# A dilated 15-tap convolution with gates: the taps split 2 apart as well, the products joined in PSUM, and a planned order

## The chip, the cores and the metric

The kernel runs on one core of one Trainium2 chip. The metric is the device time of one execution in microseconds, from the runs of the kernel by itself; beside them one execution was taken by the profiler, and the times of single instructions come from that one. The engines are named as in the profile: PE multiplies matrices (PEld is its load of the stationary operand), DVE does element-wise work, ACT applies functions and copies, POOL fills constants and issues some transfers, and SP issues most transfers.

## The reference

Cut to what is computed (two sequences of 16000 tokens with 144 channels; 15 taps, two tokens apart; all in bfloat16):

```python
B, T, D, K = (2, 16000, 144, 15)
pad = (K - 1) * 2
xp = jnp.pad(x, ((0, 0), (pad, 0), (0, 0)))
h = sum(einsum('btc,cd->btd', xp[:, pad - 2*i : pad - 2*i + T, :], w[i]) for i in range(K))
z = tanh(h[..., :D]) * sigmoid(h[..., D:])
return z @ w_o
```

Since the taps are two tokens apart, the even and the odd tokens are two sequences of their own, each with 15 neighbouring taps.

## The kernel before

**Tiling.** A stretch is 24 positions of one parity. A block is 64 stretches of both parities, which makes 128 rows: ten blocks and a half one. A unit is 12 of the 24 positions of the 128 stretches (`r` is 0 or 1), 21 units in all. For each unit the stationary operand of every matmul is a 128x128 piece of the input (128 channels by 128 stretches) and the moving one is a tap's weights, 128x288; the results stand in PSUM as 128 stretches by 288 outputs, two of them in an `acc` of two banks.

**Split taps.** The taps 8 apart are split in the manner of Karatsuba, so that the input appears as four streams, S (sum of two positions 8 apart), D (their difference) and E twice (the difference 16 apart, for the products that the code numbers 2 and 3). Each stream is split once more, 4 apart: `pe_V` makes a shared product with summed weights `H` (8 matmuls), `pe_A` makes the four others from the differences S4, D4 or E4 (`derive`). In each of these the 16 channels beyond 128 of up to eight taps are one more matmul, on `rx` and the weights `Wr`, `wrA` and `wrB`. That is 110 matmuls of 288 columns in a unit. ACT takes every product from PSUM to SBUF (`ev_V`, `act_ev`), and DVE adds the shared product to the others (`tt` with `bc`) and sums the products to `y`, for the last two products straight from PSUM.

**The rest of a unit.** `gate_act` and `gate_mul` make `z`. A transposing transfer on SP's queue makes `zT` of it (`start_zT`), and in the following unit PE multiplies it by `w_o` (`outproj`, four groups of 6 matmuls of 144 columns), ACT copies the groups to `os`, and SP stores them.

**Loads.** For a block SP issues four transposing loads (`load_x`: `xn` holds channels 0 to 127, `xb` channels 16 to 143), and then eight copies within SBUF that shift the last 16 channels of `xb` by 0 to 7 positions into `rx` (`load_r`).

**Order.** Every instruction stands in the order in which the code is written (`keep_in_program_order`). Weights come over ACT's queue (L191) and POOL's, and DVE makes their sums (L225 to L239). PE is kept busy with 54 matmuls on zeros (L218) until the first data are there. The transfers of SP and ACT take eight completion semaphores in turn (DMAHW0 to DMAHW7), those of POOL eight others (DMASW0 to DMASW7). A transfer is issued only after the earlier transfer on the same semaphore has landed, and while it waits, everything behind it on the issuing engine waits too. The first places of ACT's order are these; `[waits ...]` names the semaphores that end a wait:

```order
L191 DMA w_all<-in_w_dram 128x4x288 x3
L191 DMA w_all<-in_w_dram 128x3x288
L194 ACT_TABLE_LOAD
L194 ACTIVATE warm<-warm 128x1 [waits Pool_49]
L245 COPY H<-w_all 128x288 [waits DMAHW4_49]
L247 ACTIVATE Wr<-wrA 128x288 [waits DMASW0_49]
```

ACT issues four transfers here, none of which waits, and then goes over to its own work.

Of the kernel before, what the change touches and what calls it, by code (L numbers as in the profile page):

```python
# [8 lines left out]
BF16 = mybir.dt.bfloat16  # L9
# [4 lines left out]

@with_exitstack
def kernel(
# [7 lines left out]

    nc = tc.nc
    P = 128
# [3 lines left out]
    CM = 128  # L39
    CR = D - CM  # L40
    PU = 24
    NCL = 12
    HA = 16
    GAP = 32
    assert (B, T, D, K, D2) == (2, 16000, 144, 15, 288)
    TOT = 2 * T + GAP
    NBIG = 10
    BTOK = [3072] * NBIG + [1536]
    BT0 = [3072 * i for i in range(NBIG + 1)]
    NBLK = NBIG + 1  # L50
    assert BT0[-1] + BTOK[-1] >= TOT
    XW = HA + 1536 + 16
    ZW = 1792

# [4 lines left out]
    xa_pool = ctx.enter_context(tc.tile_pool(name="xa", bufs=2))  # L59
    d_pool = ctx.enter_context(tc.tile_pool(name="d", bufs=2))  # L60
    y_pool = ctx.enter_context(tc.tile_pool(name="y", bufs=2))
    c_pool = ctx.enter_context(tc.tile_pool(name="c", bufs=2))
    v_pool = ctx.enter_context(tc.tile_pool(name="v", bufs=4))
    g_pool = ctx.enter_context(tc.tile_pool(name="g", bufs=2))
    zt_pool = ctx.enter_context(tc.tile_pool(name="zt", bufs=2))
    os_pool = ctx.enter_context(tc.tile_pool(name="os", bufs=2))
    ps_acc = ctx.enter_context(tc.tile_pool(name="ps_acc", bufs=3, space=bass.MemoryType.PSUM))
    ps_out = ctx.enter_context(tc.tile_pool(name="ps_out", bufs=2, space=bass.MemoryType.PSUM))


    def segs(bi):

        t0 = BT0[bi] - 2 * HA
        t1 = BT0[bi] + BTOK[bi]
        loads, zeros = [], []
        marks = [(-2 * HA, 0, None, 0), (0, T, 0, 0), (T, T + GAP, None, 0), (T + GAP, TOT, 1, T + GAP),
                 (TOT, TOT + 1536, None, 0)]
        for (a, e, b, base) in marks:
            a_, e_ = max(a, t0), min(e, t1)
            if a_ >= e_:  # L80
                continue
            c0, c1 = (a_ - t0) // 2, (e_ - t0) // 2
            if b is None:
                zeros.append((c0, c1))
            else:
                loads.append((c0, b, a_ - base, c1 - c0))
        return loads, zeros

    def store_segs(bi):

        res = []
        p0, npd = BT0[bi] // 48, BTOK[bi] // 48
        for b in range(B):
            f0 = (b * (T + GAP)) // 48
            nfull, rest = T // 48, (T % 48) // 4
            a, e = max(f0, p0), min(f0 + nfull, p0 + npd)
            if a < e:
                res.append((a - p0, e - a, NCL, b, (a - f0) * 48))
            if rest and p0 <= f0 + nfull < p0 + npd:
                res.append((f0 + nfull - p0, 1, rest, b, nfull * 48))  # L100
        return res

    blocks = {}

    def load_x(bi, names=("xn", "xb")):
        loads, zeros = segs(bi)
        cur = blocks.setdefault(bi, dict(bi=bi))
        for nm in names:
            c0 = 0 if nm == "xn" else D - P
            t_ = xa_pool.tile([P, 2, XW], BF16, name=nm)  # L110
            cur[nm] = t_
            for (a, e) in zeros:
                K_(nc.gpsimd.memset(t_[:, :, a:e], 0.0))
            for e in range(2):
                for (col, b, tk, n) in loads:
                    src = bass.AP(x.tensor, x[b, tk + e, c0].offset, [[2 * D, n], [1, P]])
                    K_(nc.sync.dma_start_transpose(out=t_[:, e, col:col + n], in_=src))  # L117

    def load_r(bi, engs=None):
        engs = engs or (nc.sync,)  # L120
        cur = blocks[bi]
        cw = HA + BTOK[bi] // 2
        rx = xa_pool.tile([P, 2, XW], BF16, name="rx")
        for i in range(8):
            K_(engs[i % len(engs)].dma_start(out=rx[CR * i:CR * (i + 1), :, 8:cw], in_=cur["xb"][P - CR:P, :, 8 - i:cw - i]))  # L125
        cur["rx"] = rx

    def tt(out_, a, b, op):
        return K_(nc.vector.tensor_tensor(out=out_, in0=a, in1=b, op=op))  # L129


    GEO = {"S": (-8, 16), "D": (-8, 16), "E": (-16, 24), "S4": (-8, 12), "D4": (-8, 12), "E4": (-16, 20),
           "Sr": (0, 8), "Dr": (0, 8), "Er": (-8, 16)}

    def derive(bi, nm):
        cur = blocks[bi]
        big = bi < NBIG
        npd = BTOK[bi] // 48
        u0, wd = GEO[nm]
        t_ = d_pool.tile([P, GEO[nm][1] * P], BF16, name=nm)  # L140
        cur[nm] = t_

        def src(x_, u):

            s = u + HA
            v = x_[:, :, s:s + PU * npd]
            if big and wd == PU:
                return v
            return v.rearrange("p e (k j) -> p e k j" if big else "p e (k j) -> p j e k", j=PU)[
                (slice(None),) * (3 if big else 1) + (slice(0, wd),)]  # L150

        if nm in ("S4", "D4", "E4"):
            b = cur[nm[0]]
            bw = GEO[nm[0]][1]
            if big:
# [382 lines left out]
```

## Time and profile before

| | us |
|---|---|
| three runs by themselves | 354.19, 352.77, 353.88 (median 353.88) |
| span of the profiled execution | 352.6 |
| PE busy in it | 334.4 (95%) |
| weight loads on PE | 318.0 (90%) |
| DVE, ACT busy | 293.2 (83%), 220.8 (63%) |

The span of the profiled execution is 1.3 us below the median of the runs. A row of the groups view names the line, the engine, the operation, output and inputs, the shape and the count; behind the bar stand busy time, the mean of one in ns, and the idle time before. A row of the chain of waits has start, duration and what the chain ran through. `L267` is the line of every matmul and `L129` that of every DVE operation on two tensors, so their tiles tell them apart: `acc` is the convolution, `po` the output product.

### The profile page before, as it was taken

Reading aid. Unit: us, or ns where it says so; the run is one execution under the profiler, and the core shown is the slowest. Engines: PE = TensorE matmul, PEld = TensorE weight load, DVE = VectorE, ACT = ScalarE, POOL = GpSimd, SP = SyncE. Lnnn points to the kernel's source line nnn. Section 1 sums busy time; section 2 is a strip of 40 time slices with the busy share of each in tenths; the row PEclk is TensorE's granted clock in tenths of the full one; section 3 lists DMA queues with packets and bytes.
Section 4 is the critical chain, followed back from the end, with each engine's and each line's share of the span. In section 5 each row is a group of like instructions: output and inputs, shape, how many; then the busy total and the mean of one; then the engine's idle time right before and its main releaser. Section 6 shows DMA issues by size and latency. Waiting matters only on the chain.

```text
span 352.6 us, 7171 instructions
## 1 busy us (share of the span) xinstructions
PE 334.4 (95%) x2891; PEld 318.0 (90%) x2892; DVE 293.2 (83%) x393; ACT 220.8 (63%) x388; POOL 21.3 (6%) x48
## 2 busy tenths in 40 slices
PE   8938899999999999989999999989999999999994
PEld 3527799999999999989999999989999999999873
DVE  1826999789889888977988897878889889979984
ACT  2122567576765767657576765757676575776773
POOL 5255100000000000000000000000000000000002
PEclk9987999999999999999999999999999999999999
DMA  9998899969869787697997888698789865633224
GB/s 203 132 119 181 89 157 148 120 131 180 129 97 196 145 91 145 110 162 110 196 151 94 161 122 137 86 187 168 92 169 159 121 116 90 121 73 60 59 46 93
DMA packets 141881, 45.33 MB, mean 129 GB/s; under 512 B 136938, under 2 KB 139306, under 8 KB 141848
## 3 DMA queue, kind: packets, MB, share of 16 engines
q1 hardware_dynamic: 138588, 42.28, 73.6%
q0 software_dynamic: 1024, 1.43, 3.1%
q10 hardware_dynamic: 2236, 1.17, 1.3%
q8 instruction: 22, 0.36, 0.4%
q14 instruction: 11, 0.09, 0.1%
HBM read 1.62 MB, written 9.22 MB: 31 GB/s over the span
## 4 chain that ended last, share of the span: by engine, by line
PE 83%; DMA 9%; SPq 3%; DVE 2%; POOL 1%; ACT 1%; issue 0%; ACTq 0%; POOLq 0%
PE acc L267 74%; PE po L267 9%; DMA zT<-z 6%; SPq L117 3%; DMA wo_ab<-in_w_o_dram 2%; DMA xb<-in_x_dram 1%; DVE y L129 1%; POOL rx L125 1%; DVE m L129 0%; POOL wo_ab L211 0%; POOL wo_ab L212 0%; PE acc L359 0%; DVE mm L129 0%; DVE u L129 0%; DVE Sr L129 0%
## 5 line engine op out<-in xcount | busy, mean ns | idle before, releaser
L267 PEld LDWEIGHTS <-E 128*128 128x128 bf16 x966 | 117.5, 144 | 2.8 <-issue 1.8
L267 PE MATMUL acc<-w_all,E 128*128 128x288 bf16 x630 | 101.3, 286 | 1.7 <-DVE y L129 1.7
L329 ACT CAST os<-po 128x432 bf16<-128x432 f32 x80 | 41.4, 517 | 59.6 <-PE po L267 59.5
L267 PEld LDWEIGHTS <-S 128*128 128x128 bf16 x504 | 62.7, 142 | 1.6
L291 ACT ACTIVATE v<-acc 128x576 bf16<-128x576 f32 x84 | 52.4, 649 | 18.4 <-PE acc L267 18.4
L267 PEld LDWEIGHTS <-D 128*128 128x128 bf16 x504 | 63.2, 141 | 0.6
L267 PE MATMUL acc<-G,S 128*128 128x288 bf16 x294 | 49.4, 291 | 0.0
L267 PE MATMUL acc<-Gm,D 128*128 128x288 bf16 x294 | 48.0, 286 | 0.0
L306 ACT ACTIVATE th<-y 128x576 bf16<-128x576 bf16 (+1 forms) x64 | 43.4, 678 | 4.9 <-DVE y L129 4.9
L267 PE MATMUL po<-wo_ab,zT 128*128 128x144 bf16 x480 | 43.1, 226 | 3.2 <-DMA zT<-z 3.2
L267 PE MATMUL acc<-H,E 128*128 128x288 bf16 x336 | 44.6, 286 | 0.0
L307 ACT ACTIVATE sg<-y 128x576 bf16<-128x576 bf16 (+1 forms) x64 | 43.0, 672 | 0.0
L291 ACT ACTIVATE mm<-acc 128x576 bf16<-128x576 f32 x42 | 27.4, 652 | 24.1 <-PE acc L267 24.1
L267 PEld LDWEIGHTS <-zT 128*128 128x128 bf16 x480 | 35.3, 98 | 6.2 <-DMA zT<-z 4.3
L129 DVE TENSOR_TENSOR y<-m,acc 128x576 bf16<-128x576 bf16 x42 | 31.3, 752 | 8.5 <-PE acc L267 8.1
L129 DVE TENSOR_TENSOR m<-m,v 128x1152 bf16<-128x1152 bf16 x42 | 31.7, 755 | 3.6 <-ACT m L291 1.5
L129 DVE TENSOR_TENSOR z<-th,sg 128x576 bf16<-128x576 bf16 (+1 forms) x64 | 28.8, 449 | 6.3 <-ACT sg L307 5.3
L291 ACT ACTIVATE m<-acc 128x576 bf16<-128x576 f32 x42 | 26.9, 654 | 9.5 <-PE acc L267 9.5
L129 DVE TENSOR_TENSOR y<-u,acc 128x576 bf16<-128x576 bf16 x42 | 31.4, 748 | 0.6 <-PE acc L267 0.5
L267 PE MATMUL acc<-Wr,Sr 128*128 128x288 bf16 x84 | 24.5, 292 | 7.1 <-DVE Sr L129 7.1
L129 DVE TENSOR_TENSOR mm<-mm,v 128x1152 bf16<-128x1152 bf16 x21 | 15.9, 758 | 16.3 <-ACT mm L291 16.2
L267 PEld LDWEIGHTS <-Er 128*128 128x128 bf16 x168 | 24.2, 144 | 0.2
(65 smaller groups left out, 396.3 us busy)
## 6 DMA issues: line engine op xcount, KB each, us to landing
out_dram<-os SPq DMA_DIRECT2D x36, 216.0 KB
rx<-xb SPq DMA_DIRECT2D x72, 96.5 KB
w_all<-in_w_dram ACTq DMA_DIRECT2D x3, 288.0 KB
rx<-xb POOLq DMA_DIRECT2D x8, 96.5 KB, 5.6
out_dram<-os SPq DMA_DIRECT2D x4, 168.8 KB
rx<-xb SPq DMA_DIRECT2D x8, 48.5 KB
xn<-in_x_dram SPq DMA_TRANSPOSE x24
xb<-in_x_dram SPq DMA_TRANSPOSE x24
```

The lines of the kernel that those rows point to most:

```text
L117: K_(nc.sync.dma_start_transpose(out=t_[:, e, col:col + n], in_=src))
L125: K_(engs[i % len(engs)].dma_start(out=rx[CR * i:CR * (i + 1), :, 8:cw], in_=cur["xb"][P - CR:P, :, 8 - i:cw - i]))
L129: return K_(nc.vector.tensor_tensor(out=out_, in0=a, in1=b, op=op))
L267: K_(nc.tensor.matmul(ps, lhsT=l, rhs=r, start=(k == 0), stop=(k == n - 1)))
L291: K_(nc.scalar.activation(out=dst, in_=acc[:, :, 0:D2], func=ACT.Copy, scale=sign))
L306: K_(nc.scalar.activation(out=th[:, 0:n], in_=y[:, c0:c0 + n, 0:D], func=ACT.Tanh))
L307: K_(nc.scalar.activation(out=sg[:, 0:n], in_=y[:, c0:c0 + n, D:D2], func=ACT.Sigmoid))
L329: K_(nc.scalar.copy(out=cur["os"][:, 3 * g:3 * g + 3, :].rearrange("p a d -> p (a d)"), in_=po[:, 0:3 * D]))
```

## The change

- **One more split.** S4, D4 and E4 become sums of positions 4 apart instead of differences, and the weights of the shared products differences instead of sums. The shared product of each stream is itself split, for taps 2 apart: S2, D2 and E2 are sums of positions 2 apart, `HH` are differences of the weights `H`. `VV` (2 matmuls), `V2a` and `V2b` (2 each) take the place of the 8 of `pe_V`. A unit has 102 matmuls of 288 columns, and 24 of 144 as before.
- **Sums finished in PSUM.** ACT copies the negated `VV` from the first bank of a pair X to its second (`cVV`, 288 elements), PE adds `V2a` and `V2b` on top, ACT copies the negated pair X to a pair Y (`cV`, 576 elements), and PE adds the four products on top of X and Y. ACT then takes the pairs of S and D to `m`, and DVE adds those of E to `U` straight from PSUM. DVE no longer adds shared products. Pairs of banks are four slots, used in turn by the convolution, by the output product and by the weights' sums.
- **Blocks of one parity.** A block is 128 stretches of one parity, and S, D, S2, D2, Sr and Dr have one buffer each.
- **The last 16 channels.** SP copies them from `x` to `xr`, a tensor in DRAM with 16 channels in a row (`gather`, eight copies of 32-byte pieces, 32000 pieces in all), and `rx` is a transposing load of overlapping windows of `xr` (`load_r`). ACT's queue fills the gaps of `xr` with zeros and loads `Wr` in 15 copies.
- **Weights' sums.** Those of S come from PE, with an identity as stationary operand, and ACT copies them out (`psum_sum`); D's come from DVE, and Wr's from POOL.
- **Order.** A planner (`Plan.place`) lays out each engine's steps ahead of the build: it takes, among the steps that can start earliest on an engine, the one with the least `want`, with costs per step that stand in the code. The transfers are not held to that order by `keep_in_program_order`.
- **Output.** Results of four units stand together in `os`, and rows of 24 tokens are stored at once. The last block is stored by 12 transfers on SP (`store_last`; 4 for the later half of the columns, 8 for the earlier half).

```diff
-    def pe_V(cur, m):
-        acc = ps_acc.tile([P, 2, 512], F32, name="acc")
-        for b1 in range(2):
-            mm_bank(acc[:, b1, 0:D2], [(stat(cur, NM[m], SH[m] + 2 * b1 - i), H[:, m, i, :]) for i in range(4)])
-        return acc
...
-    def quad(name):
-        return c_pool.tile([P, 2, 2, D2], BF16, name=name)
...
-        act_ev(mm_[:, 1], pe_A(cur, 1, 1), 0.5)
-        act_ev(mm_[:, 0], pe_A(cur, 1, 0), -0.5)
-        tt(mm_[:], mm_[:], bc(vm), ALU.add)
...
+                low = min(st for st, _ in cand) + self.WAIT.get(e, 0.0)
+                st, s = min((c for c in cand if c[0] <= low), key=lambda c: (c[1].want, c[1].idx))
+                if pick is None or st < pick[0]:
+                    pick = (st, s)
...
+    def gather(key, p0, n, planes, want):
+        g = xr_g[key] = Gen()
+        loads, _ = runs(p0, n)
+        for c, b, p, m in loads:
+            e0, ne = planes[0], len(planes)
+            src = bass.AP(x.tensor, x[b, 2 * p + e0, P].offset, [[2 * D, m], [D, ne], [1, CR]])
+            dst = bass.AP(xr.tensor, xr[e0, FRONT + p0 + c, 0].offset, [[CR, m], [NPOS * CR, ne], [1, CR]])
+            add("DMA", m * ne * 0.0013, lambda dst=dst, src=src: nc.sync.dma_start(out=dst, in_=src), w=[g], want=want, name="gather")
...
+    def load_r(bi, want, keys):
+        p0, n, planes, _ = geometry(bi)
+        g = blk[bi]["rx"] = rx_b.new(bi)
+        for i, e in enumerate(planes):
+            v = plane(g.tile, bi, i)
+            src = bass.AP(xr.tensor, xr[e, FRONT + p0 - HA - 7, 0].offset, [[CR, HA + n], [1, P]])
+            add("DMA", (HA + n) * 0.0015, lambda v=v, src=src: nc.sync.dma_start_transpose(out=v, in_=src),
+                r=[gz, *(xr_g[k] for k in keys)], w=[g], want=want, name="rx")
...
+    gz = Gen()
+    for q, (p0, m) in enumerate(((-FRONT, FRONT), (HP, GAP), (ENDP, NPOS - FRONT - ENDP))):
+        dst = bass.AP(xr.tensor, xr[0, FRONT + p0, 0].offset, [[P, m * CR // P], [NPOS * CR, 2], [1, P]])
+        add("ACT", 0.08, lambda dst=dst, m=m: nc.scalar.dma_start(out=dst, in_=zr[0:m * CR // P]), w=[gz], want=-30.5 if q == 0 else -25, lat=2.5)
...
+    for q, (t0, t1) in enumerate(((0, 4), (4, 8), (8, 12), (12, K))):
+        add("ACT", 0.08, lambda t0=t0, t1=t1: nc.scalar.dma_start(out=w_all[:, t0:t1, :], in_=w[t0:t1, 0:P, :].rearrange("k c d -> c k d")),
+            w=[gw[q]], want=-31 + q, lat=5.0 + 1.5 * q)
...
+    for k, j0, m in (("F", 0, 8), ("G", 8, 7)):
+        for j in range(m):
+            c = P - CR * (j + 1)
+            add("ACT", 0.08, lambda k=k, j=j0 + j, c=c: nc.scalar.dma_start(out=Wr[c:c + CR, KI[k], :], in_=w[j, P:D, :]), w=[gWr[k]], want=-27, lat=4.0)
...
+        psum_sum(HH[:, i], [plus(i, j) + minus(i, j + 4) + minus(i, j + 2) + plus(i, j + 6) for j in range(2)], wall, [gHH[k]], wt)
...
+    add("ACT", 0.35, lambda: K_(nc.scalar.copy(out=H[:, 3, 3, :], in_=w_all[:, 11, :])), r=[gw[2]], w=[gH["G"]], want=-4)
+    for k, want in (("F", -20), ("G", -12)):
+        wsum(HH[:, KI[k]], H[:, KI[k], 0:2], H[:, KI[k], 2:4], ALU.subtract, [gH[k]], [gHH[k]], want)
...
+        add("PE", t_pe(D2, 2), lambda: run(X, 0, [job(st, v - i, HH[:, i4, i, :]) for i in range(2)], True),
+            r=[g[st], gHH[k]], w=[a], want=base + AT["VV" + k], opens=X, pairs=[X], behind=[last_open[0]] if last_open[0] else [], name="VV" + k)
+        add("ACT", t_act(D2), lambda: K_(nc.scalar.activation(out=banks[X.slot][:, 1, 0:D2], in_=banks[X.slot][:, 0, 0:D2], func=ACT.Copy, scale=-1.0)),
+            r=[a], w=[b], want=base + AT["VV" + k] + 0.3, pairs=[X], name="cVV" + k)
+        add("PE", t_pe(D2, 2), lambda: run(X, 0, [job(st + "2", v - 2 - i, H[:, i4, i + 2, :]) for i in range(2)]),
+            r=[g[st + "2"], gH[k]], u=[a], want=base + AT["V2" + k], pairs=[X], name="V2a" + k)
+        add("PE", t_pe(D2, 2), lambda: run(X, 1, [job(st + "2", v - i, H[:, i4, i, :]) for i in range(2)]),
+            r=[g[st + "2"], gH[k]], u=[b], want=base + AT["V2" + k] + .01, pairs=[X], name="V2b" + k)
+        s = add("ACT", t_act(2 * D2), lambda: K_(nc.scalar.activation(out=banks[Y.slot][:, :, 0:D2], in_=banks[X.slot][:, :, 0:D2], func=ACT.Copy, scale=-1.0)),
+                r=[a, b], w=[*Y.part], want=base + AT["V2" + k] + DUR["V2" + k], pairs=[X, Y], opens=Y, name="cV" + k)
+        last_open[0] = s
+        for b2, pair in enumerate((X, Y)):
...
+        for b2, pair in enumerate((X, Y)):
+            for c in range(2):
+                jobs = []
+                for i in range(4):
+                    wt = tap(k, i if b2 else i + 4)
+                    if wt is not None:
+                        jobs.append(job(st + "4", v + 2 * c - i - (0 if b2 else 4), wt))
+                rest = [job(st + "r", v + 2 * c + 4 * b2, Wr[:, i4, :])]
...
+            for i, k in enumerate("SD"):
+                for b2, pair in enumerate(conv(bi, r, k, base, AT)):
+                    add("ACT", t_act(2 * D2), lambda pair=pair, i=i, b2=b2: K_(nc.scalar.activation(
+                        out=m.tile[:, i, 2 * b2:2 * b2 + 2, :], in_=banks[pair.slot][:, :, 0:D2], func=ACT.Copy, scale=0.5)),
+                        r=[*pair.part], w=[m], want=done(k, b2) + .2, pairs=[pair], name=f"ev{b2}{k}")
...
+            add("DVE", t_dve(4 * D2), lambda: tt(y.tile[:, 4:8, :], m.tile[:, 0], m.tile[:, 1], ALU.subtract),
+                r=[m], w=[*gens(4, 4), y], want=done("D", 1) + .8, name="y1")
+            add("DVE", t_dve(4 * D2), lambda: tt(U.tile[:], m.tile[:, 0], m.tile[:, 1], ALU.add), r=[m], w=[U], want=done("D", 1) + 1.5, name="U")
+            gate(4, 4, done("D", 1) + 1.5)
...
+        for r in range(2):
+            for e in range(2):
+                for row, n, m, b, t0 in store_rows(NMB * P, 32):
+                    c0, c1 = 6 * h, min(6 * h + 6, m // 4)
+                    if c0 >= c1:
+                        continue
+                    dst = bass.AP(out.tensor, out[b, t0 + 4 * c0 + 2 * r + e, 0].offset, [[48 * D, n], [4 * D, c1 - c0], [1, D]])
+                    s0 = 64 * r + 32 * e + row
+                    src = os.tile[s0:s0 + n, 0:c1 - c0, :]
+                    add("DMA", 0.3, lambda dst=dst, src=src: K_(nc.sync.dma_start(out=dst, in_=src)), r=[os], want=want, name="store")
...
+    for s in plan.place():
+        s.fn()
...
```

**ACT's first places, after the change** (ahead of them stand three loads of `w_all` and the zero fill of `xr`; more Wr rows of the same kind between them are left out):

```order
L364 DMA w_all_90<-in_w_dram 128x3x288 [waits DMAHW0_49]
L370 DMA Wr_95<-in_w_dram 16x288 [waits DMAHW1_49]
...
L370 DMA Wr_95<-in_w_dram 16x288 [waits DMAHW5_49]
L370 DMA Wr_95<-in_w_dram 16x288 [waits DMAHW6_49,Pool_49]
L361 DMA xr_71<-zr_102 2x2x128 [waits DMAHW7_49]
L361 DMA xr_71<-zr_102 14x2x128 [waits DMAHW0_49]
L433 COPY H_93<-w_all_90 128x288
L401 COPY HH_94<-acc0_63 128x576 [waits PE_49]
```

ACT now issues 22 transfers, and its first copy of weights stands behind the last of them.

**SP's first places, after the change** (xn0 and rx0 belong to the first block, xn1 and rx1 to the second; an xr row is a gather):

```order
L244 DMA_TRANSPOSE xn1_68<-in_x_dram 128x3072
L262 DMA_TRANSPOSE rx0_69<-xr_71 128x3088 [waits DMAHW4_49,DMAHW3_49,DMAHW2_49]
L254 DMA xr_71<-in_x_dram 3072x16 [waits DMAHW1_49]
L254 DMA xr_71<-in_x_dram 3072x2x16 [waits DMAHW3_49]
L254 DMA xr_71<-in_x_dram 1856x2x16 [waits DMAHW5_49]
L254 DMA xr_71<-in_x_dram 1200x2x16 [waits DMAHW7_49]
```

A transfer's own semaphore is among those it waits for, so these rows and ACT's show who holds whom. The load of rx0 is on DMAHW3, and the gather of 3072x2 on DMAHW3 stands behind it. The gathers of 1856x2 and 1200x2 are on DMAHW5 and DMAHW7, and the next users of these two are ACT's Wr row with DMAHW5 and ACT's xr row with DMAHW7.

**DVE's first places, after the change** (E0, E20 and E40 are the E, E2 and E4 of the first block):

```order
L383 TENSOR_TENSOR H_93<-w_all_90 128x864 [waits DMAHW0_49]
L383 TENSOR_TENSOR HH_94<-H_93 128x576 [waits DVE_49,Activation_49]
L271 TENSOR_TENSOR E0_74<-xn0_67 128x1536 [waits DMAHW3_49]
L271 TENSOR_TENSOR E20_84<-E0_74 128x1792 [waits DVE_49]
L271 TENSOR_TENSOR E40_80<-E0_74 128x2560
L271 TENSOR_TENSOR S0_72<-xn0_67 128x2048
```

The second half of E, and all that is derived from the input after it, now stands behind an HH that waits for ACT's copy of L433.

**PE in one of the units in the middle, after the change** (`H,D` is the last of V2b of D, `HH,E` is VV of a product of E, `Gm,D` begins the products of D on top of its X; the rows left out repeat these):

```order
L319 LDWEIGHTS D20_83
L319 MATMUL acc3_66<-H_93,D20_83 128x288
...
L319 LDWEIGHTS E1_75
L319 MATMUL acc1_64<-HH_94,E1_75 128x288
...
L319 LDWEIGHTS D41_79
L319 MATMUL acc3_66<-Gm_92,D41_79 128x288
```

Between V2b of D, after which ACT makes `cV`, and the products that wait for `cV`, two matmuls stand here, as in seven of the 21 units. In most others twelve stand there: the ten on the second pair of S as well.

More of the change, by code (lines that the diff above doesn't have):

```diff
@@ L89, in store_segs @@
[L89 to L126, printed above, removed]
+    psum = ctx.enter_context(tc.tile_pool(name="psum", bufs=1, space=bass.MemoryType.PSUM))
+    dram = ctx.enter_context(tc.tile_pool(name="dram", bufs=1, space=bass.MemoryType.DRAM))
```

823 lines of the change are left out of this document (478 added, 345 removed).

## The prediction

> **What bounds the kernel now.** I read the shares of busy time first, then the chain of waits, then the waits.
>
> ```profile
> PE 334.4 (95%) x2891; PEld 318.0 (90%) x2892; DVE 293.2 (83%) x393; ACT 220.8 (63%) x388; POOL 21.3 (6%) x48
> PEclk9987999999999999999999999999999999999999
> PE 83%; DMA 9%; SPq 3%; DVE 2%; POOL 1%; ACT 1%; issue 0%; ACTq 0%; POOLq 0%
> ```
>
> PE is busy nearly throughout, at full clock but for one place near the start, and carries 83% of the chain. The chain in order of time shows three stages:
>
> ```profile
> 10.72 4.39 DMA xb<-in_x_dram
> ...
> 20.17 6.51 DMA wo_ab<-in_w_o_dram
> 26.68 0.69 DVE Sr L129
> 27.42 6.30 PE acc L267 x36
> ...
> 55.25 10.05 PE acc L267 x82
> 65.30 0.38 PE po L267 x6
> ...
> 70.24 10.05 PE acc L267 x82
> ...
> 343.76 0.99 PE acc L267 x8
> ...
> 348.53 0.40 ACT os L373
> ```
>
> A start of 27.4 us is bound by transfers. Then a unit takes 14.99 us (55.25 to 70.24), with PE never idle: 110 matmuls at 10.05 / 82 = 0.1226 us and four groups at 0.38. From PE's last convolution matmul (344.75) to the last copy (348.93) 4.2 us pass, and 3.7 us more to the end of the span. PE alone decides the middle, transfers the start, and a chain of short steps the end.
>
> ```profile
> PEld L267 <- DMA zT<-z: 4.3, 4, 1.3
> PE acc L267 <- DVE Sr L129: 7.1, 1, 7.1
> POOL wo_ab L212 <- DMA rx<-xb: 2.3, 2, 1.2
> ```
>
> The first row is all that the middle loses, about 4 us in four waits for zT; the second is PE's pause in the start. The third matters for the change: the load of wo_ab reads nothing of rx, yet POOL waits for rx to land before it issues it. The wait on a reused completion semaphore is real, and it holds the issuing engine.
>
> **The middle.** Eight matmuls go, so a unit costs PE 102 x 0.1226 + 24 x 0.063 = 14.0 us, 0.98 less. That holds if ACT and DVE keep up.
>
> ```profile
> L291 ACT ACTIVATE v<-acc 128x576 bf16<-128x576 f32 x84 | 52.4, 649 | 18.4 <-PE acc L267 18.4
> L329 ACT CAST os<-po 128x432 bf16<-128x432 f32 x80 | 41.4, 517 | 59.6 <-PE po L267 59.5
> L306 ACT ACTIVATE th<-y 128x576 bf16<-128x576 bf16 x62 | 42.5, 686 | 4.7 <-DVE y L129 4.7
> L248 ACT ACTIVATE Wr<-Wr 128x288 bf16<-128x288 bf16 x2 | 0.8, 433 | 0.0
> L129 DVE TENSOR_TENSOR y<-u,acc 128x576 bf16<-128x576 bf16 x42 | 31.4, 748 | 0.6 <-PE acc L267 0.5
> 13.47 1.22 DVE L129 TENSOR_TENSOR S<-xn 128x2048 bf16<-128x2048 bf16 x1
> 14.61 1.22 DVE L129 TENSOR_TENSOR D<-xn 128x2048 bf16<-128x2048 bf16 x1
> 15.74 1.75 DVE L129 TENSOR_TENSOR E<-xn 128x3072 bf16<-128x3072 bf16 x1
> 17.41 0.60 DVE L129 TENSOR_TENSOR H<-w_all 128x864 bf16<-128x864 bf16 x1
> 40.08 0.69 ACT L306 ACTIVATE th<-y 128x576 bf16<-128x576 bf16 x1 [2.82 <-DVE y L129]
> 40.67 0.67 ACT L307 ACTIVATE sg<-y 128x576 bf16<-128x576 bf16 x1
> 41.08 1.14 PE L267 MATMUL acc<-H,D 128*128 128x288 bf16 x8
> 42.32 0.65 ACT L291 ACTIVATE v<-acc 128x576 bf16<-128x576 f32 x1 [0.32 <-PE acc L267]
> ```
>
> ACT's unit: 4 cVV at 0.43, 8 copies of 576 at 0.65 (4 cV, 4 to m), 6 gates at 0.69, and two copies of 864 at 0.91 (0.517 for 432, and 432 more at the 0.92 ns per element between 432 and 576). Sum 12.9 us, below 14.0, and less where they follow closely (th to sg, 0.59 from start to start). The trace has no copy from PSUM to PSUM; I take the row from PSUM to SBUF. DVE's pitch, from the rows at 13 to 17 us, is 0.065 us and 0.5225 ns per element (2048 in 1.13, 3072 in 1.67). The derived tiles of a block (20224 elements in 12 instructions) cost 11.3 us, half of it per unit; with 4 y at 0.75, y1 and U at 0.67 and three z at 0.37 a unit has 11.1 us. Both fit, so PE remains the bound.
>
> Where the order is tight PE waits. In seven units `cV` of D has only two matmuls to hide behind: ACT first copies the second pair of S (0.59 to the next start), then makes cV (0.65); with 0.1 to begin (PE ends at 42.22, ACT starts at 42.32) that is 1.34 us after the pair's last matmul, and PE has 6 matmuls in it (0.74 us). So 0.6 us each, 4.2 us in all. Elsewhere twelve matmuls (1.47 us) cover about 0.8 us of V2, start and cV. The four zT waits go, since the output product now stands about a unit later.
>
> **The start.** Now what ACT waits for. Its first copy of weights stands behind 22 issues. The Wr row on DMAHW5 waits for the gather of 1856x2, the xr row on DMAHW7 for the gather of 1200x2. SP issues both only after the gather on DMAHW3, and this one only after rx0 has landed. So ACT, which copied weights at 8.25 us before, is held until rx0 and then four gathers are through. DVE stops at the HH that needs ACT's copy, and PE after its first four slots. The prices:
>
> ```profile
> 8.25 0.43 ACT L245 COPY H<-w_all 128x288 bf16<-128x288 bf16 x1 [3.82 <-DMA w_all<-in_w_dram]
> q1 hardware_dynamic: 4937, 1.24, 117.8%
> q1 hardware_dynamic: 1568, 0.44, 72.3%
> q1 hardware_dynamic: 138588, 42.28, 73.6%
> q10 hardware_dynamic: 2236, 1.17, 1.3%
> 0.75 2.15 ACTq L191 DMA_DIRECT2D w_all<-in_w_dram  x4
> 46.54 4.11 SPq L117 DMA_TRANSPOSE xn<-in_x_dram  x2
> 55.83 1.33 SPq L348 DMA_DIRECT2D out_dram<-os  x2
> out_dram<-os POOLq DMA_DIRECT2D x4, 30.4 KB, 2.1
> ```
>
> The second row is the stretch 48 to 53 us, transposing loads alone: 4937 packets of 256 bytes in 5 us, 1.01 ns each over all engines (117.8% x 80 us / 4937 = 19.1 ns on one). The third is 57 to 60 us, stores of 288 bytes: 22.1 ns. Weights (q10): 33 ns for 523 bytes. Issue alone costs SP 1.3 ns per row (4.11 us for 3104 rows) or 0.87 (1.33 us for 1536 pieces). A gather moves 32 bytes per packet, DRAM to DRAM; no row shows that. Below, the line through 256 and 523 bytes gives 7.7 ns at 32, or 0.41 over all engines; above, the mean packet of the whole queue is 30.0 ns, or 1.6. I take 1.1, between the two prices of issue, since a piece costs an issue whatever its size.
>
> Before, four loads of 6144 rows with the weights beside them had landed at 15.1 us. Now the first gather (3072 x 1.1 = 3.4) and rx0 (3088 x 1.1 = 3.4) come on top: 21.9. The gathers behind it, 3072 + 6144 + 3712 + 2400 = 15328 pieces, take 16.9 us, their landing 2 and ACT's last two issues 1.1 (2.15 / 4 each). The first of them overlaps rx0's landing, 0.5 less. ACT is free at **41.4 us**; at 28.7 with the low price (18400 pieces x 0.69 ns less), at 50.6 with the high one.
>
> From there DVE decides: copy of H (0.43), then HH, E, E2, E4, S, Er and on to D of the second block, 23 instructions of 35392 elements, 23 x 0.065 + 18.5 = 20.0 us, plus about 1 us in S2 and D of that block, which wait until PE's VV and V2 of the second unit have read the single buffers. PE does its unit beside that: 110 matmuls are 13.5 us and, from the row of 36 in 6.30 us after the 7.1 us pause, 1.9 us lost to the lower clock. Then y1, U and two y (4 x 0.67), and the last gates: th and sg after the last y are queued among six (0.6 each from start to start), 1.9 us behind it, and only then ACT makes cV of D in the second unit (0.65). PE's first product of D there starts at 41.4 + 0.4 + 21 + 2.7 + 1.9 + 0.7 = 68.1. By then 136 of 2142 convolution matmuls are done.
>
> **The end.** The chain after the last matmul is as before (4.2 us). But SP alone issues the last eight stores, where SP and ACT shared four:
>
> ```profile
> 206.99 5.04 SPq L348 DMA_DIRECT2D out_dram<-os  x6
> 343.87 6.51 SPq L348 DMA_DIRECT2D out_dram<-os  x8
> 348.96 1.03 ACTq L348 DMA_DIRECT2D out_dram<-os  x2
> ```
>
> SP's row ends at 350.38, 2.2 us before the span. Eight issues at 0.66 (1.33 / 2) are 5.3, so the end is 4.2 + 5.3 + 2.2 = 11.7 instead of 7.9; at ACT's 0.52 it is 10.6, at the 0.84 of the six in the first row 13.1.
>
> **The sum.** 68.1 + 2006 x 0.1226 (245.9) + 480 x 0.063 (30.2) + 4.2 + 11.7 = 360.1 us of span, against 352.6. With the 1.3 us between span and median: **361 us**, 2% slower. The middle gains 19.6 + 4 - 4.2 us, the end loses 3.8, and the start some 23. The gathers' bounds are 349 and 371; no stalls at all would take off 4, and the same stall in every unit add 8.
>
> **The rivals.** (1) *Cheap gathers.* A packet of 32 bytes costs what the line through the two sizes says, 0.41 ns. Then ACT is free at 28.7 and the time is 348.7, faster by 1.5%. It decides below 0.6 ns, where the time is 0.5% under the old one. For it: bytes do matter between 256 and 523. Against: 288-byte stores lie above that line, and so do the prices of issue. [...] No run here shows a 32-byte piece. Chance 0.20.
>
> (2) *Dear gathers*, DRAM at both ends, 1.6 ns: 9 us more, 371 and above. For it: the stores, which end in DRAM, cost more than loads of nearly the same size. Chance 0.10.
>
> (3) *ACT sets the pace of the middle.* 12.9 of 14.0 us leaves little; if each unit loses 0.6 as the seven do, 8 us more, 369. Against: its issue pitch is shorter than its means (0.57 for 0.65), so it has some 3 us free. Chance 0.08.
>
> (4) *ACT isn't held*: the transfers it waits for land before it comes to them, and the start is as long as before: about 340. Against: the order of the semaphores leaves no way round rx0. Chance 0.04.
>
> My own forecast, 353 to 368, has 0.58. With a measurement that can't tell less than 0.5% from no change (352.1 to 355.7), rivals 1 and 4 and the lowest end of the forecast make faster 0.24; same 0.08; slower 0.68. The range that leaves out 2 in 10 is 347 to 371; the likeliest case alone 353 to 368.
>
> **What would show it.** ACT's first copy (L433) at 38 to 45 us, with the last Wr and xr issues ending as the gathers land; PE idle from its first sums until then and at a lower clock after; a unit of 14.0 us with PE full in the middle, 14.6 in seven; no wait for zT; eight stores on SP after the last copy. ACT's first copy below 32 us, or units over 14.6 us, would make the forecast wrong, the first downwards and the second upwards.

## The result: 4.7% slower, and where the time lies

The changed kernel takes 370.0 us (median of four runs, 369.88 to 371.7), the kernel before 354.03 on the same chip: a ratio of 1.047, with a 95% interval of 1.042 to 1.052. The profiled execution has a span of 368.1 us.

The first page of the kernel after, its shares of busy time, the granted clock and the chain of waits:

```profile
PE 325.8 (89%) x2762; PEld 303.6 (82%) x2762; DVE 251.1 (68%) x338; ACT 246.7 (67%) x440; POOL 15.6 (4%) x36
PEclk9965998999999999999999999999999999999997
PE 39%; DVE 26%; ACT 13%; DMA 12%; issue 7%; SPq 2%; ACTq 0%; DVEq 0%
```

PE does 129 matmuls less and is busy 9 us less, but its share falls from 95% to 89%, and it carries 39% of the chain where it carried 83%. DVE and ACT now hold 39% of it between them: PE often waits for a short step of theirs.

To see where, I cut both executions at the same two places: the start of the 137th convolution matmul (after the change it is the first product of D in the second unit) and the end of the last one. The rows of PE for these places, of the kernel before and then of the kernel after (start, duration, what it is, and in brackets how long PE stood idle and for what):

```profile
43.28 0.53 PE L267 MATMUL acc<-G,S 128*128 128x288 bf16 x3
...
344.46 0.29 PE L267 MATMUL acc<-Wr,Er 128*128 128x288 bf16 x1
```

```profile
54.28 0.41 PE L319 MATMUL acc<-HH,E 128*128 128x288 bf16 x2
58.33 0.53 PE L319 MATMUL acc<-Gm,D 128*128 128x288 bf16 x3 [3.64 <-ACT acc L489]
...
355.98 0.29 PE L319 MATMUL acc<-Wr,Er 128*128 128x288 bf16 x1
```

Between the two places PE's work is its matmuls by their pitch (0.1226 us for 288 columns, 0.063 for 144). The rest are gaps: whatever the starts of two matmuls lie further apart than the pitch. Summed over the trace:

| us | start | PE's work | gaps | end | span |
|---|---|---|---|---|---|
| before | 43.3 | 296.9 | 4.5 | 7.8 | 352.6 |
| after | 58.3 | 276.3 | 21.6 | 11.8 | 368.1 |
| difference | +15.1 | -20.6 | +17.1 | +4.0 | +15.5 |

So the change gives what it says, 20.6 us of PE's work, and pays for it three times. Of the 21.6 us of gaps, 13.2 lie at VV, V2 and the products behind them, where PE waits for ACT's `cVV`, `cV` or a freed pair of banks; 6.6 lie ahead of output products; 1.6 are a stretch at half the clock (58.91 to 62.32, granted clock 0.50). (The gaps by kind are summed in the same way for the experiments below.)

**The start.** ACT's queue and SP's in the kernel after (ACTq and SPq rows are issues of transfers, waits between them included):

```profile
15.79 13.20 ACTq L370 DMA_DIRECT2D Wr<-in_w_dram  x11
29.75 0.68 ACTq L361 DMA_DIRECT2D xr<-zr  x2
30.46 0.43 ACT L433 COPY H<-w_all 128x288 bf16<-128x288 bf16 x1 [27.73 <-DMA xr<-zr]
```

```profile
12.49 3.30 SPq L262 DMA_TRANSPOSE rx<-xr  x1
15.84 2.77 SPq L254 DMA_DIRECT2D xr<-in_x_dram  x2
...
18.02 9.03 SPq L254 DMA_DIRECT2D xr<-in_x_dram  x4
```

After warming up, ACT does no work of its own until 30.46, right behind its last two issues, the zero fills of `xr`, of which the first stands behind the gather of 1200x2 (landed at 29.73). SP's second gather of this stretch goes out at 18.02, when rx0 has landed. This is the mechanism of the forecast, but it lets go at 30.5 and not at 41.4. The packets of the window from 21 to 27 us, when almost nothing but gathers moves (packets, MB, share of the engines' time):

```profile
q1 hardware_dynamic: 9254, 0.30, 149.4%
```

9254 packets of 32 bytes in 6 us are 0.65 ns a piece.

One thing about the kernel before, on which the prediction's row of POOL rests: in the first two blocks POOL issues four of the eight copies to `rx` itself, and SP the other four. The load of `wo_ab` that waits for rx waits for one of POOL's own copies, on the same semaphore.

**The middle.** One of the units in which the order is tight, PE's rows and then ACT's of the same stretch:

```profile
131.86 0.29 PE L319 MATMUL acc<-Wr,Sr 128*128 128x288 bf16 x1
132.29 0.65 PE L319 MATMUL acc<-H,D 128*128 128x288 bf16 x4 [0.15 <-ACT acc L483]
132.86 0.41 PE L319 MATMUL acc<-HH,E 128*128 128x288 bf16 x2
133.94 0.53 PE L319 MATMUL acc<-Gm,D 128*128 128x288 bf16 x3 [0.67 <-ACT acc L489]
```

```profile
131.83 0.41 ACT L483 ACTIVATE acc<-acc 128x288 f32<-128x288 f32 x1
132.16 1.19 ACT L544 ACTIVATE m<-acc 128x576 bf16<-128x576 f32 x2
133.22 0.67 ACT L489 ACTIVATE acc<-acc 128x576 f32<-128x576 f32 x1
```

Before V2 of D (132.29) PE waits for `cVV`: a matmul started at 131.86, the next 0.43 later, so a gap of 0.31. Behind it, two matmuls of VV later, it waits for `cV`, which ACT starts only when it has copied both pairs of S to `m`: 132.98 to 133.94, a gap of 0.83. The same two gaps come back in six units, and the longer one in a seventh. The waits of the kernel after (us in all, times, the longest):

```profile
DVE y L271 <- ACT m L544: 44.5, 10, 4.8
DVE Dr L271 <- PE acc L319: 18.1, 10, 2.9
PEld L319 <- DMA zT<-z: 4.8, 6, 1.4
```

The waits for zT have not gone; the loads of the stationary operand wait for it six times where they did four times.

### The profile page after: what moved, and what is told of

Read it like the earlier page. It is cut to its first block, busy times and chain, and to the rows that moved or that the text cites. A ratio compares the mean times of both kernels' runs of the same rounds, so it can differ in the third digit from the quotient of the medians.

```text
span 368.1 us, 6824 instructions
## 1 busy us (share of the span) xinstructions
PE 325.8 (89%) x2762; PEld 303.6 (82%) x2762; DVE 251.1 (68%) x338; ACT 246.7 (67%) x440; POOL 15.6 (4%) x36
## 4 chain that ended last, share of the span: by engine, by line
PE 39%; DVE 26%; ACT 13%; DMA 12%; issue 7%; SPq 2%; ACTq 0%; DVEq 0%
PE acc L319 39%; DVE y L271 9%; DMA zT<-z 6%; DVE S L271 5%; DVE E L271 4%; DMA xr<-in_x_dram 4%; ACT os L632 3%; ACT acc L489 2%; ACT m L544 2%; DVE z L271 2%; ACT th L526 2%; ACT sg L528 2%; DMA rx<-xr 1%; DVE U L271 1%; DVE Dr L271 1%
## 5 line engine op out<-in xcount | busy, mean ns | idle before, releaser
L544 ACT ACTIVATE m<-acc 128x576 bf16<-128x576 f32 x84 | 53.6, 647 | 29.0 <-PE acc L319 28.5
L319 PEld LDWEIGHTS <-D 128*128 128x128 bf16 x462 | 58.7, 138 | 16.3 <-issue 14.1
L271 DVE TENSOR_TENSOR y<-U,acc 128x576 bf16<-128x576 bf16 x80 | 60.0, 750 | 14.5 <-PE acc L319 12.3
L489 ACT ACTIVATE acc<-acc 128x576 f32<-128x576 f32 x84 | 53.9, 642 | 5.2 <-PE acc L319 4.2
L319 PE MATMUL acc<-Wr,Er 128*128 128x288 bf16 x168 | 47.4, 286 | 0.0
L271 DVE TENSOR_TENSOR y<-m 128x1152 bf16<-128x1152 bf16 x21 | 15.9, 757 | 44.5 <-ACT m L544 44.5
L483 ACT ACTIVATE acc<-acc 128x288 f32<-128x288 f32 x84 | 33.7, 402 | 12.2 <-PE acc L319 12.0
L319 PE MATMUL acc<-wo_ab,zT 128*128 128x144 bf16 x480 | 35.9, 226 | 5.0 <-DMA zT<-z 3.2
L632 ACT CAST os<-acc 128x864 bf16<-128x864 f32 x40 | 34.3, 872 | 3.8 <-PE acc L319 3.6
L319 PE MATMUL acc<-H,E 128*128 128x288 bf16 x168 | 28.1, 290 | 0.5 <-ACT acc L483 0.5
L271 DVE TENSOR_TENSOR E<-E 128x1792 bf16<-128x1792 bf16 (+3 forms) x22 | 26.4, 1234 | 0.0
```

The lines of the kernel that those rows point to most:

```text
L319: K_(nc.tensor.matmul(bank, lhsT=l(), rhs=r, start=start and q == 0, stop=end and q == len(jobs) - 1, skip_group_check=True))
L483: add("ACT", t_act(D2), lambda: K_(nc.scalar.activation(out=banks[X.slot][:, 1, 0:D2], in_=banks[X.slot][:, 0, 0:D2], func=ACT.Copy, scale ...
L489: s = add("ACT", t_act(2 * D2), lambda: K_(nc.scalar.activation(out=banks[Y.slot][:, :, 0:D2], in_=banks[X.slot][:, :, 0:D2], func=ACT.Cop ...
L544: add("ACT", t_act(2 * D2), lambda pair=pair, i=i, b2=b2: K_(nc.scalar.activation(out=m.tile[:, i, 2 * b2:2 * b2 + 2, :], in_=banks[pair.s ...
L632: K_(nc.scalar.copy(out=dst, in_=banks[pr.slot][:, :, 0:3 * D].rearrange("p h (q d) -> p h q d", d=D)))
```

## The experiments

Each kernel changes the kernel after, and each is timed beside the kernel before (353.9 to 354.3 us). The ratios are to that kernel, so the kernel after stands at 1.047. The planner lays out every kernel anew, so an edit can move steps that it does not name. In the table, "V" are the gaps at VV, V2 and the products behind them, "output" those ahead of output products.

| us | median | ratio (95%) | start | V | output | all gaps | end |
|---|---|---|---|---|---|---|---|
| after | 370.0 | 1.047 (1.042-1.052) | 58.3 | 13.2 | 6.6 | 21.6 | 11.8 |
| wr_on_pool | 358.9 | 1.014 (1.011-1.017) | 42.9 | 13.1 | 11.0 | 26.0 | 12.3 |
| zt_own_queue | 361.3 | 1.022 (1.018-1.025) | 58.7 | 7.8 | 2.3 | 12.0 | 11.8 |
| cover_d | 365.8 | 1.034 (1.030-1.038) | 59.8 | 9.6 | 5.2 | 15.1 | 11.8 |
| tail_two_queues | 369.9 | 1.043 (1.038-1.048) | 58.5 | 13.4 | 6.3 | 19.6 | 10.2 |
| start_and_order | 352.2 | 0.993 (0.991-0.996) | 42.8 | 8.2 | 8.5 | 19.1 | 12.3 |
| dr_two_buffers | 362.8 | 1.025 (1.021-1.030) | 60.2 | 7.3 | 2.0 | 15.2 | 11.8 |
| order_tail_dr | 353.3 | 0.998 (0.995-1.001) | 43.5 | 6.9 | 5.3 | 18.1 | 10.7 |
| half_sums | 354.4 | 0.999 (0.996-1.002) | 43.4 | 4.2 | 7.6 | 20.9 | 10.9 |
| order_tail | 352.1 | 0.993 (0.991-0.996) | 42.9 | 8.2 | 10.2 | 21.5 | 10.9 |
| zt_before_load | 346.1 | 0.977 (0.973-0.981) | 42.5 | 7.8 | 4.5 | 13.9 | 10.7 |

**wr_on_pool: ACT's queue freed.**

```diff
-            add("ACT", 0.08, lambda ...: nc.scalar.dma_start(out=Wr[c:c + CR, KI[k], :], ...
+            add("POOL", 0.8, lambda ...: nc.gpsimd.dma_start(out=Wr[c:c + CR, KI[k], :], ...
```

The last two zero fills of `xr`, which ACT still issues, are planned a little earlier as well (`want` -27.5 for -25).

> The 15 small loads of Wr are issued by POOL instead of ACT, so that ACT's first copy of weights stands behind 7 issues instead of 22. Theory A (the start is lost because ACT's queue stands behind completion semaphores that the gathers reuse): ACT's first copy moves from 30.5 us to about 13 us, the first product of D in the second unit from 58.3 to 42-46 us, and the whole time falls by 11 to 16 us, to 354-359. Rival B (the start is bound by the transfers themselves, rx1 and the gathers, and ACT's wait only lies beside them): ACT's copy comes early, but DVE and PE then wait for xn1 and rx1, and the time falls by less than 4 us. The middle should keep its 22 us of PE gaps in both.

```profile
5.37 4.38 ACTq L361 DMA_DIRECT2D xr<-zr  x2
9.80 0.43 ACT L433 COPY H<-w_all 128x288 bf16<-128x288 bf16 x1 [7.06 <-DMA xr<-zr]
```

ACT's own timeline of this run: the copy comes at 9.80, and the start falls by 15.4 us, to 42.9, as theory A has it. That is as early as the kernel before has its 137th matmul, so ACT's queue accounts for the whole loss of the start. The time falls by 11.1 us only, since 4.4 us come back as waits ahead of output products, and the middle's other gaps stay.

**zt_own_queue: another planned order.** In the planner's model zT stood behind the modelled loads on one queue; now it has a queue of its own there. On the chip it is SP as before.

```diff
+SEM = {..., "DMA": 2.2, "ZQ": 2.2}
-            add("DMA", 2.7, lambda: K_(nc.sync.dma_start_transpose(out=zT.tile[:], ...
+            add("ZQ", 2.7, lambda: K_(nc.sync.dma_start_transpose(out=zT.tile[:], ..., lat=3.8,
```

> Only the planner's picture changes: the transposes of z get a queue of their own in its model (2.7 us and 3.8 us until they are seen), instead of standing behind the modelled loads. The instructions are the same, their order on PE, ACT, DVE and SP is another: every unit but the first ones has VV of D, ten products of S, V2 of D, ten products of S, VV of F, products of D, and the output products stand behind the products of F. Theory A (the middle loses 17.7 us more than forecast because the planned order leaves too little between V2 and the products, and puts output products ahead of zT's landing): the gaps of PE after 58 us fall from 22 us to 5-10, the time by 11 to 16 us. Rival B (ACT and DVE set the pace, and the gaps only show where it comes out): the gaps move to other places of the unit, the unit stays at 14.6-14.9 us, and the time changes by less than 4 us.

The gaps fall from 21.6 to 12.0 us and the time by 8.7, between the two theories and nearer to A. PE's rows where a unit used to be tight:

```profile
130.73 0.65 PE L319 MATMUL acc<-H,D 128*128 128x288 bf16 x4
131.22 0.65 PE L319 MATMUL acc<-G,S 128*128 128x288 bf16 x4
131.71 0.29 PE L319 MATMUL acc<-Wr,Sr 128*128 128x288 bf16 x1
131.84 0.65 PE L319 MATMUL acc<-G,S 128*128 128x288 bf16 x4
132.33 0.28 PE L319 MATMUL acc<-Wr,Sr 128*128 128x288 bf16 x1
132.45 0.41 PE L319 MATMUL acc<-HH,E 128*128 128x288 bf16 x2
132.69 0.53 PE L319 MATMUL acc<-Gm,D 128*128 128x288 bf16 x3
```

With twelve matmuls from V2 of D to D's products (ten of S and two of VV) there is no gap left. In the next unit, the second of the block, there is one still, and ACT's rows tell why:

```profile
144.94 0.69 ACT L526 ACTIVATE th<-y 128x576 bf16<-128x576 bf16 x1 [0.74 <-DVE y L271]
145.53 0.67 ACT L528 ACTIVATE sg<-y 128x576 bf16<-128x576 bf16 x1
146.10 0.63 ACT L544 ACTIVATE m<-acc 128x576 bf16<-128x576 f32 x1
146.63 0.64 ACT L489 ACTIVATE acc<-acc 128x576 f32<-128x576 f32 x1
```

DVE's y is late, so both gates stand ahead of the copy to `m` (which frees the pair that VV needs at 146.78) and of `cV` (for which the products wait until 147.33). That is two gaps of 0.30 in every other unit, whatever the cover. Here rival B is right: ACT's queue sets them.

**cover_d: only the cover.** Five products of S are put behind V2 of D by a rule in the planner, and nothing else is asked of it.

```diff
+        if k == "D" and base > 0:
+            last_a1[0][0].behind.add(vv)
+            last_a1[0][1].behind.update((vv, v2))
```

> The planner is only told that in every unit VV of D starts before the last ten products of S, and V2 of D before the last five. So 5 products of S stand between V2 of D and the products of D where it was 2 matmuls of VV only (7 units), 7 matmuls (0.86 us) in all. Theory A (gaps there are the missing cover): the six gaps of 0.83 us shrink to 0.3 each, the waits for zT stay, the time falls by 2 to 4 us. Rival B (ACT is late there for a reason of its own, its queue of copies, so that cover doesn't help): the gap stays within 0.2 us of 0.83 and the time within 1 us.

The gaps of 0.83 shrink to 0.30, as theory A says, V falls by 3.6 us and the time by 4.2. Part of that is chance: this execution had no stretch at half the clock behind its start (worth 1.6 us; mean granted clock 0.974, in the kernel after 0.969), and its start came 1.4 later.

**tail_two_queues.**

```diff
-                    add("DMA", 0.3, lambda dst=dst, src=src: K_(nc.sync.dma_start(out=dst, in_=src)), ...
+                    q = h == 0 and e == 1
+                    add(("DMA", "ACT")[q], 0.3, lambda ..., q=(nc.sync, nc.scalar)[q]: K_(q.dma_start(out=dst, in_=src)), ...
```

> Four of the last eight stores go out on ACT's queue instead of SP's. Theory A (the end is SP issuing eight stores one after the other, some 0.57 us each): the stretch from the last copy to the end falls from 6.7 us to 4.3-4.8, the time by 2 to 2.4 us. Rival B (the end is the landing of the last stores, whichever queue issues them): less than 0.7 us.

In the trace the end is 10.2 instead of 11.8 us. The time doesn't show it: one run took 366.5 us, the other three 369.7 to 370.1, and the one is the profiled run, which had no stretch at half the clock after its start either (granted clock 1.00 from 40 to 70 us; worth 1.6 us). The stretch is shorter by 1.6, less than theory A says; a gain in the time isn't shown.

**start_and_order: both together** (the edits of wr_on_pool and zt_own_queue).

> wr_on_pool and zt_own_queue together. Theory A (start and middle are separate losses): ACT's first copy at about 10 us, the first product of D in the second unit at 43 us as in wr_on_pool, the gaps behind it 12 us as in zt_own_queue, so 361.3 - 15.6 = 346 us (344.5-348), 2% below the kernel before the change. Rival B (the early start meets data that have not landed, as the 4.4 us that wr_on_pool lost at zT): 349-352 us.

352.2 us, and that is where theory B's range ends: start and V are where they should be, but 8.5 us of gaps stand ahead of output products. It is faster than the kernel before all the same, by 0.7%. The largest of these gaps, 4.7 us, is the first zT; zt_before_load comes back to it.

**dr_two_buffers.** zt_own_queue with "Dr" among the names that have two buffers.

> zt_own_queue, and Dr gets a second buffer, so that DVE need not wait for PE's last reading of the old Dr (18 us of DVE's time in 10 waits), with y and U queued behind it. Theory A (that wait delays y, the gates and so cV): the gaps of PE behind V2 and VV fall from 7.8 us to 3-4, the time from 361.3 to 356-358.5. Rival B (the gaps of 0.3 come from y standing behind the long sums of the next block in DVE's order, in the other unit of each pair): DVE's wait goes, PE's gaps stay, 360-362.

362.8 us, no faster than zt_own_queue (361.3) and a little above rival B's 360 to 362, and yet the test doesn't decide. DVE's wait was 18.4 us in zt_own_queue and is still 14.1:

```profile
DVE Dr L271 <- PE acc L319: 14.1, 8, 1.8
```

The planner starts whatever can start. With two buffers it moved each Dr a block ahead, to where the second buffer was about to come free, and DVE waits there. What y would gain without that wait is open.

**order_tail_dr and half_sums.** The first is start_and_order with both of these edits, the second has the sums of blocks 1 to 9 in halves as well.

> start_and_order, with Dr's second buffer and with four of the last eight stores on ACT's queue. If the tail is worth what its trace showed (1.6 us) and Dr what theory A of dr_two_buffers says (3-5), 340-343 us; if Dr is worth nothing, 344-346; if neither, 346-348.

> order_tail_dr, and the sums S, D, S4, D4, Sr, Dr and E, E4, Er of the blocks 1 to 9 are made in two halves of 64 stretches each, so that no sum on DVE that y may stand behind is longer than 0.9 us (1.75 before). Theory A (the remaining gaps of 0.3 us are y behind a long sum): PE's gaps behind V2 and VV fall by 3 us or more against order_tail_dr, the time by 2-4 us. Rival B (ACT's queue of gates and copies is what is late, whatever DVE does): the gaps stay, and the time is within 1 us of order_tail_dr or up to 1 us above it, for some 80 more instructions on DVE at 0.065 us.

353.3 and 354.4 us: neither is better than start_and_order, and order_tail_dr misses all three of its forecasts, which counted from 346 us. The second buffer for Dr brings something of its own: all three kernels that have it, and no other, show a gap of 3.2 us in the last blocks; with what comes behind it, that makes 4.1 us of other gaps in dr_two_buffers and in order_tail_dr. In dr_two_buffers the matmuls there come at about twice the pitch: the first three behind the idle time (3.08 us) take 0.88 us and not 0.53. The halves take V from 6.9 to 4.2, not quite the 3 us of theory A, which fits long sums ahead of y as a part of these gaps; the plan moved too, so it is not shown. Other gaps grow by 5.5 us, at output products and elsewhere, and the time doesn't fall.

**order_tail** (start_and_order with the divided tail) **and zt_before_load**, in which SP's load of x for the fourth block stands behind the first zT (this load is also held in the written order by `keep_in_program_order`; that line is left out here):

```diff
+                for s in plan.steps[n0:]:
+                    if s.name == "xn":
+                        s.behind.update(first_z)
```

> start_and_order with four of the last eight stores on ACT's queue, Dr with its one buffer again. Theory A (the end is SP's issuing): the end falls from 12.3 to 10.7 us as in order_tail_dr, the time from 352.2 to 350-351. Rival B (what the tail saves the last landings take back): 351.7-352.7.

> order_tail, and on SP the load of x of the fourth block stands behind the first transpose of z instead of ahead of it. Theory A (PE waits 4.7 us for the first zT because SP, one queue in order, is still issuing loads of 3 to 4 us each when z is complete): the first zT is issued 3.4 us earlier, PE's wait falls to 1-2 us, the time to 346.5-348.5. Rival B (the wait is z itself, or the output weights' landing): the wait stays above 4 us, the time within 0.7 us of order_tail. The load, 3.4 us later, should not be missed before the second unit of the third block.

order_tail's end is 1.4 us shorter than start_and_order's, its time the same (352.1 and 352.2), rival B by the number; in its profiled execution PE's first wait for zT was 1.8 us longer still, so whether the landings took the gain back is open. SP's rows, of order_tail and then of zt_before_load:

```profile
42.71 3.99 SPq L244 DMA_TRANSPOSE xn<-in_x_dram  x1
46.79 3.50 SPq L262 DMA_TRANSPOSE rx<-xr  x1
50.39 3.68 SPq L244 DMA_TRANSPOSE xn<-in_x_dram  x1
54.16 1.56 SPq L577 DMA_TRANSPOSE zT<-z  x1
```

```profile
45.22 3.48 SPq L262 DMA_TRANSPOSE rx<-xr  x1
48.80 2.25 SPq L577 DMA_TRANSPOSE zT<-z  x1
51.15 3.89 SPq L244 DMA_TRANSPOSE xn<-in_x_dram  x1
```

SP's issue of one load lasts 3.5 to 4 us, and zT stands behind three of them. DVE's z, from which it is made, is through at 43.7 in order_tail:

```profile
42.48 1.19 DVE L271 TENSOR_TENSOR z<-th,sg 128x576 bf16<-128x576 bf16 x3
```

With one load moved, PE's rows at the first output product (order_tail, zt_before_load):

```profile
58.42 0.90 PE L319 MATMUL acc<-wo_ab,zT 128*128 128x144 bf16 x6 [6.37 <-DMA zT<-z]
```

```profile
53.21 0.92 PE L319 MATMUL acc<-wo_ab,zT 128*128 128x144 bf16 x12 [1.67 <-DMA zT<-z]
```

346.06 us, a ratio of 0.977 (0.973 to 0.981): theory A, a little below its 346.5 to 348.5, and a version that beats the kernel before by 2.3% and the changed one by 6.5% (346.06 against 370.0). The time fell by 6.0 us, the wait by 4.7. The clock has a part in it: behind its long wait order_tail ran at half the clock from 56.4 to 63.2 (granted clock 0.82 and 0.84 in the windows 50 to 60 and 60 to 70, 1.00 in both in zt_before_load), which by the pitches cost 2.3 us. PE's matmuls carry 60% of the chain now. Its page:

```profile
PE 321.1 (93%) x2762; PEld 302.3 (88%) x2762; DVE 250.5 (73%) x338; ACT 245.4 (71%) x440; POOL 21.7 (6%) x51
```

## Why the prediction was right and wrong

361 us was forecast and 370.0 measured: the side was right, and so was the mechanism of the start, but the change costs 16 us and not 7. Term by term:

| us | forecast | measured |
|---|---|---|
| ACT's first copy of weights | 41.4 | 30.5 |
| from there to D of the second unit | 26.7 | 27.9 |
| PE's work behind that | 276.1 | 276.3 |
| stalls in the middle | 4.2 | 21.6 |
| the end | 11.7 | 11.8 |
| span | 360.1 | 368.1 |

- **ACT's queue held by reused semaphores: right.** ACT does no copy until rx0 and four gathers are through, and wr_on_pool shows what that costs: 15.4 us of start.
- **The gathers: mis-sized, 10.9 us too much.** rx0 had landed at 18.0, not 21.9, which is 3.9 of it. The 15328 pieces behind it were forecast at 1.1 ns, a value between two prices of issue; the trace shows 0.65 in the window above, and these pieces were through 7 us earlier. The argument "a piece costs an issue whatever its size" fell: SP issues the gather of 3072x2, 6144 pieces, within 0.6 us (18.02 to 18.6 in the rows above), far below the 0.87 ns per piece that I took as the least: 0.1 ns. The two smaller gathers behind it, 3712 and 2400 pieces, then held SP for 3.87 and 2.59 us, 1.04 and 1.08 ns a piece, so these two issues lasted as long as if they were paid by the piece; what SP waits for in them is open. The line through two packet sizes, 0.41 ns, is below the 0.65 of the trace. By the forecast's own working, ACT's copy at 30.5 alone would have made the time about 350, between rival 1 and my own range.
- **The chain of DVE from there, and PE's work: right** to 1.2 and 0.2 us. That a unit needs 14.0 us of PE holds; with its gaps it takes 14.7 (two units from the tight spot at 133.94 to the next at 163.39 take 29.45).
- **The stalls in the middle: mis-sized, and this is the step that failed.** I gave 0.6 us to seven units and nothing to the rest, 4.2 in all; it is 21.6. Four things were missed. (a) A tight unit loses 1.15, not 0.6: ACT had both pairs of S to copy ahead of `cV` and not one, and `cVV` has too little cover too (0.32). (b) Twelve matmuls of cover were called enough; they are where ACT is free, but in the second unit of a block the gates come late and stand ahead of the copies, and PE loses two times 0.30. These are most of V's 13.2 us. (c) "The four zT waits go" was wrong: the output products stand 5.0 to 11.5 us behind the issue of their zT, not a unit (14.0), and 6.6 us are lost ahead of them, 4.8 for zT and 1.8 for a late y (last section). (d) 1.6 us at half the clock.
- **ACT as the pace of the middle** (rival 3, 8 us, chance 0.08) came near in its result, 369, but by luck: its sum has the start 9.8 us too late, and the gaps grew by 17.4 us, not by 8. Only a part of it is true. With the other order (zt_own_queue) 9.6 of the 21.6 us go without one instruction of ACT less; what stays, 0.6 in every other unit, is ACT's queue. *Dear gathers* (rival 2, 371 and above) came as near, at 1.6 ns a piece where the trace shows 0.65, and *ACT isn't held* (rival 4) fell with the first point.
- **The end: right in its sum**, 11.8 against 11.7, with two errors that cancel: from PE's last convolution matmul to the last copy 5.1 us instead of 4.2, SP's eight issues 4.6 instead of 5.3, and 2.1 behind them instead of 2.2. That four of them on ACT's queue would save 2 us didn't hold: the stretch gains 1.4 to 1.6, the time nothing that could be told.

The two errors are of opposite sign, and so the range of 347 to 371 held the time for a wrong reason, by luck: its upper end was the dear gather, and not the stalls. Both signs that the prediction named for its being wrong came, ACT's first copy below 32 us and units over 14.6.

## What to carry to other kernels

Where a planner's table sets the order, the cost of a tight spot is read from all that the waiting engine has queued ahead of the awaited step, in each kind of unit; a sum over busy times ("12.9 of 14.0 us") does not show it. A transfer that is issued in order costs its queue as long as the issue lasts, so a short, urgent one (zT, 1.6 us) belongs ahead of long ones (loads of 3.5 to 4; one of them moved took 4.7 us off PE's wait in zt_before_load), and small loads don't belong on the queue of an engine that has work to begin (15 of Wr on ACT's queue; the start 15.4 us earlier without them in wr_on_pool). A gain on the bound engine is worth only what the start, the waits and the end leave of it: here 20.6 us of PE's work became a loss of 16, and two changes of the plan and two of queues made it a gain of 8.

## What the runs showed of the hardware that was not expected

**Half the clock after a pause.** Behind the pause of 3.64 us before the second unit's D, five matmuls still come at the full pitch, and the next 14 at 0.24 us and not at 0.1226: from 58.91 to 62.32, for 3.41 us, the granted clock is 0.50, and it is 1.00 in the 3.41 us before and after. In tail_two_queues the same pause, 3.39 us long, costs nothing. Windows of 60 to 70 us in both (PE busy and its count, then further on the granted clock), the kernel after and then tail_two_queues:

```profile
60.00:70.00 10.00, 10.00 (x75) 9.19 (x74) 7.02 (x11) 6.23 (x11) 0.00 (x0) 0.88 0.57 116
```

```profile
60.00:70.00 10.00, 10.00 (x95) 9.91 (x94) 8.69 (x13) 7.01 (x13) 0.00 (x0) 1.00 0.58 120
```

A shorter pause met half the clock all the same. PE's first products of D in the second unit, in start_and_order (granted clock 0.83 in the window 40 to 50, 1.00 in 30 to 40) and then in tail_two_queues (1.00 in 50 to 60):

```profile
42.82 0.88 PE L319 MATMUL acc<-Gm,D 128*128 128x288 bf16 x3 [3.15 <-ACT acc L489]
```

```profile
58.52 0.53 PE L319 MATMUL acc<-Gm,D 128*128 128x288 bf16 x3 [3.39 <-ACT acc L489]
```

Behind 3.15 us of idle time three matmuls take 0.88 us, in wr_on_pool as in start_and_order, and behind 3.39 us they take 0.53. So the length of the pause alone does not tell which it will be; what does was not shown.

**The same sum three times as dear.** DVE makes E from 1536 elements in 0.96 us in the first block and in 2.94 in the last. There the elements that follow each other in an output row stand a whole stretch apart in xn; in the other blocks they are neighbours. DVE's rows of the kernel after, and PE's beside the second of them:

```profile
5.44 0.96 DVE L271 TENSOR_TENSOR E<-xn 128x1536 bf16<-128x1536 bf16 x1 [0.50 <-DMA xn<-in_x_dram]
...
305.36 2.94 DVE L271 TENSOR_TENSOR E<-xn 128x1536 bf16<-128x1536 bf16 x1
308.23 0.73 DVE L271 TENSOR_TENSOR y<-U,acc 128x576 bf16<-128x576 bf16 x1
```

```profile
307.05 0.29 PE L319 MATMUL acc<-Wr,Er 128*128 128x288 bf16 x1
309.01 0.91 PE L319 MATMUL acc<-wo_ab,zT 128*128 128x144 bf16 x12 [1.68 <-DVE y L271]
```

The y behind the long sum is what PE's output product waits for: from 307.05 to 309.01, less one pitch, a gap of 1.84 us, part of the 6.6. The kernel before has the same long sum in its last block (2.89 us). In the last block of the kernel after, Er, which reads `rx` in the same way, takes 2.06 us for 1024 elements, and E4, whose elements are neighbours, 0.82 for 1280. That speaks for the layout as the cause; a kernel with another layout wasn't tried.
